# Holding back four chunks as two pairs with block products in a fused attention and mixer kernel

## Chip, cores and metric

The kernel runs on one core of a Trainium2 chip. The metric is device time in microseconds, the median of several executions. The four runs of the kernel before lie within 0.3% of each other, those of the changed kernel within 1.0%. All runs told here count as fast: none is more than 1.5% above the fastest run of the same kernel. The engines are TensorE (PE in the profile; PEld are its weight loads), VectorE (DVE), ScalarE (ACT), GpSimd (POOL), and the sync engine (SP), whose queue issues DMAs.

## The reference, cut to what matters

```python
# attention: 8 batches, 8 heads, 576 positions, 64 wide, with a bias by distance
scores = q @ k.T / 8 + bias[h]
attn   = softmax(scores)                       # in fp32
x      = heads_joined(attn @ v)                # (8, 576, 512)
# mixer, low rank over positions, then a feed-forward over channels
u   = x + (x.T @ U @ V).T                      # U: 576x32, V: 32x576
out = u + relu(u @ w_ch1) @ w_ch2              # 512 -> 2048 -> 512
```

## The kernel before

Attention goes by groups: a group is one pair of heads of one batch, 32 in all, numbered from 0. From group 4 on a loop runs each group in three segments. Each segment issues scores and exps, a share of feed-forward matmuls as filler, and products with v (a bias product multiplies exps by exp of the bias, on VectorE). The feed-forward works on nine chunks of 512 tokens: chunks 0 to 7 are the first 512 tokens of a batch, chunk 8 gathers the eight remainders of 64. From chunk 1 on the second product of a chunk is a block product with seven multiplications (Strassen's scheme in Winograd's form) inside a chunk; for the last two chunks together the first product is one as well.

```python
for g in range(NPAIR, NG):                     # groups 4 to 31
    for seg in range(3):
        emit_held(g, seg)                      # DMA transposes of q and k that are due
        ...                                    # scores and exps
        if 3 * g + seg < 6 * NPAIR + 5:
            work.even(6 * NPAIR + 5 - 3 * g - seg)
        else:
            work.run(2.1)                      # us of feed-forward matmuls as filler
        ...                                    # mixing, bias products, products with v
```

q and k are loaded as tiles of 128 x 512. From batch 3 on, DMA transposes on SP's queue turn them into qkT, ten for a batch. They are put into the program at a fixed place:

```python
def load_tasks(b):
    g0 = b * NPAIR
    due = max(3 * (g0 - 3) + 1, now[0] + 2)    # segments: group g0-3, its second one

def emit_held(g, seg):                         # at most two in a segment
    while held and (held[0][1] <= g or (held[0][0] <= now[0] and n < 2)):
        held.pop(0)[2]()
        n += 1
```

A relu of the first product goes to ScalarE if more than 1.5 us of filler have been issued in its segment, else to VectorE. Sums of weight blocks for the pair (fold_w1, sixteen) are made by VectorE in the last eight groups.

The softmax here doesn't subtract the row's maximum and nothing guards it: scores larger than these inputs give would overflow.

Of the kernel before, what the change touches and what calls it, by code (L numbers as in the profile page):

```python
# [36 lines left out]
def kernel(  # L37
# [34 lines left out]
    qbp = ctx.enter_context(tc.tile_pool(name="qbp", bufs=16))  # L72
# [61 lines left out]
    uT = [const.tile([128, NPAIR, S0], FP16, name=f"uT{i}") for i in range(3)]  # L134
    u_rem = const.tile([128, 4, NPAIR, 128], FP16)
    uT_rem = const.tile([128, NPAIR, S0], FP16)

    def rem_heads(t):
        return t.rearrange("p (a two d) -> p a two d", two=2, d=D)

# [114 lines left out]
    def first_cast(st, cast):  # L255
        qb = qbp.tile([128, 512], BF16, name="qb")
        cast(
            out=qb.rearrange("p (j h d) -> p h j d", j=4, h=2),
            in_=st.rearrange("p (h j d) -> p h j d", h=2, j=4),
        )  # L260
        return qb

    def first_qk(which, pr):
        qb = qbp.tile([128, 512], BF16, name="qb")
        first_load(which, 2 * pr, 2 * pr + 2, qb, nc.gpsimd)
        return qb

    def load_main(b, which, t):
        src = (q, k, v)[which]
        if which < 2:  # L270
            tl = qbp.tile([128, 512], BF16, name="qb")
            dst = tl.rearrange("p (h d) -> p h d", h=H)
        else:
            tl, dst = None, v_bf[b % 2][:, t, :, 0:64]
        nc.gpsimd.dma_start(  # L275
            out=dst,
            in_=src[b, :, t * 128 : (t + 1) * 128, :].rearrange("h p d -> p h d"),
        )
        return tl

    def load_rest(which, t):
        tl = qbp.tile([128, 512], BF16, name="qb")
        nc.gpsimd.dma_start(
            out=tl[:, 0:384].rearrange("p (h d) -> p h d", d=D),
            in_=(q, k)[which][2, 2:H, t * 128 : (t + 1) * 128, :].rearrange(
                "h p d -> p h d"
            ),
        )
        return tl

    def load_pair(b, which, pr):
        tl = qbp.tile([128, 512], BF16, name="qb")
        dst = tl.rearrange("p (j h d) -> p j h d", j=4, h=2)
        for hh in range(2):
            nc.gpsimd.dma_start(
                out=dst[:, :, hh, :],
                in_=(q, k)[which][b, 2 * pr + hh, 0:S0, :].rearrange(
                    "(t p) d -> p t d", p=128
                ),
            )  # L300
        return tl
# [103 lines left out]
    def first_product(j, tail, g, after):  # L405
        rhs = uT[j % 3] if j < B else uT_rem
        for nt in range(NHT):
            gp_ = acc()
            for ct in range(4):
                nc.tensor.matmul(  # L410
                    gp_,
                    lhsT=w1b[:, ct, nt * 128 : (nt + 1) * 128],
                    rhs=rhs[:, ct, :],
                    start=(ct == 0),
                    stop=(ct == 3),
                )
                yield MM
            if (nt % 2) if tail else clock["seg"] > 1.5:
                nc.scalar.activation(g[:, nt, :], gp_, AF.Relu)  # L419
            else:  # L420
                nc.vector.tensor_relu(out=g[:, nt, :], in_=gp_)  # L421
            after(nt)

# [4 lines left out]
    def u_of(j, i, h):  # L428
        t, a = slice(2 * i, 2 * i + 2), slice(2 * h, 2 * h + 2)
        if j < B:  # L430
            return u_tok[j % 3][:, a, t, :].rearrange("p a t c -> p t a c")
        return u_rem[:, t, a, :]
# [19 lines left out]
    def plain_chunk(j, tail):  # L452
# [3 lines left out]
        for i in range(2):  # L456
            ob = osb.tile([128, 2, DM], FP32, name="ob")
            for t in range(2):
                ps = acc()
                c0 = 256 * i + 128 * t  # L460
                for nt in range(NHT):
# [13 lines left out]
                    in1=u_tok[j % 3][:, :, 2 * i + t, :],  # L475
                    op=ALU.add,
                )
            store(j, i, ob)

# [51 lines left out]
    def second_product(j, rows, between=lambda n: None, y_first=False):  # L531
# [56 lines left out]
        add(z, blk(1, 1), u_of(j, 1, 1))  # L588
        if y_first:
            y = bank()  # L590
            between(1)
            yield from half(y[:, 0, :], "a12", "b21", 0, True)
# [9 lines left out]
        store(j, 1, ob[1])  # L602
        if j < B:
            if y_first:
                yield from half(y[:, 1, :], "a12", "b21", 1, False)
            else:
                y = bank()
                yield from product(y, "a12", "b21", True)
            more(y, 0, 0)
        else:  # L610
            store_rem(1, ob[1])
            yield from late(0)
# [3 lines left out]
        if j < B:  # L616
            store(j, 0, ob[0])
        else:
            store_rem(0, ob[0], cols=slice(256, 512))
            yield from late(1)  # L620


    w1s = {}

    def fold_w1(i):
        m, q4 = divmod(i, 4)
        kt, h = divmod(q4, 2)
        lo = slice(512 * h, 512 * h + 512)
        hi = slice(1024 + 512 * h, 1536 + 512 * h)
        a11, a21 = w1b[:, kt, lo], w1b[:, kt, hi]  # L630
        a12, a22 = w1b[:, 2 + kt, lo], w1b[:, 2 + kt, hi]
        x, y, op = (
            lambda: (a21, a22, ALU.add),
            lambda: (w1s[1, kt, h], a11, ALU.subtract),
            lambda: (a11, a21, ALU.subtract),
            lambda: (a12, w1s[2, kt, h], ALU.subtract),
        )[m]()
        t = qbp.tile([128, 512], BF16, name="qb").bitcast(FP16)
        nc.vector.tensor_tensor(out=t, in0=x, in1=y, op=op)
        w1s[m + 1, kt, h] = t  # L640

    pb7, pb8 = uT[(B - 1) % 3], uT_rem
    t12 = uT[(B - 3) % 3]
    t34 = u_tok[(B - 3) % 3].rearrange("p a t c -> p a (t c)")

    def fold_u(i, ks):
        o = slice(ks.start, ks.stop)
        b1, b2 = slice(ks.start, ks.stop), slice(2 + ks.start, 2 + ks.stop)
        t1, t2 = t12[:, b1, :], t12[:, b2, :]
        out_, x, y = (  # L650
            (t1, pb8[:, b1, :], pb7[:, b1, :]),
            (t2, pb8[:, b2, :], t1),
            (t34[:, b1, :], pb8[:, b2, :], pb8[:, b1, :]),
            (t34[:, b2, :], pb7[:, b2, :], t2),
        )[i - 1]
        nc.vector.tensor_tensor(out=out_, in0=x, in1=y, op=ALU.subtract)

    flat = [p_sb[i].rearrange("p k h c -> p (k h c)").bitcast(FP16) for i in range(2)]
# [6 lines left out]
    def pair_chunk(sixth):  # L665
# [7 lines left out]
            [], [],  # L673
            v_bf[0].rearrange("p k h c -> p (k h c)").bitcast(FP16)[
                :, 0:2048
            ].rearrange("p (n c) -> p n c", c=256),
        )
        kept = [q32[1][:, 512 * i : 512 * i + 512] for i in range(5)]
# [5 lines left out]
        second7 = []  # L684
        x, y, z = {}, {}, {}

        def block(i, kt, n):
            c0 = (n if i in (11, 12) else 8 + n) * 128
            return w1b[:, kt + (2 if i in (12, 22) else 0), c0 : c0 + 128]
# [84 lines left out]
        for i in (3, 2, 4):  # L774
            fold_u(i, slice(1, 2))
# [18 lines left out]
        rest = second_product(B - 1, rows7, between, True)  # L794
# [19 lines left out]
        yield from second_product(B, rows8)  # L814
# [7 lines left out]
    class Work:  # L822
        def __init__(self):
            self.gens = [(0, plain_chunk(0, False))]
            self.gens += [(j, chunk(j, False)) for j in range(1, B - 2)]
            sixth = chunk(B - 2, False)
            self.gens += [(B - 2, head(sixth, 161)), (B - 1, pair_chunk(sixth))]
# [4 lines left out]
        def even(self, segs):  # L832
            self.run((128 * MM - self.done) / segs)
# [261 lines left out]
    def mix_h(g, hm=None):  # L1095
        b, pr = divmod(g, NPAIR)
        x, tt = x_pr[g], tt_pr[g]
        if hm is None:
            hm = acc()
        for t in range(4):  # L1100
# [9 lines left out]
            out=u_tok[b % 3][:, pr, :, :],  # L1110
# [4 lines left out]
        if on_pe(g):  # L1115
            return
        nc.sync.dma_start_transpose(
            out=uT[b % 3][:, pr, :].rearrange("c (t p) -> c t p", p=128),
            in_=u_tok[b % 3][:, pr, :, :].rearrange("p t c -> p (t c)"),
# [5 lines left out]
    def mix_ut(g, copy):  # L1125
# [16 lines left out]
        return lambda: copy(uT[b % 3][:, pr, :], tp)  # L1142

    def mix_rem(g, hr):
# [6 lines left out]
        def post():  # L1151
# [6 lines left out]
            if b % 2 == 0:  # L1158
                return
            r = b // 2  # L1160
            if b < B - 1:
                if pr < NPAIR - 1:
                    return
                prs = slice(0, NPAIR)
            elif pr == 0:
                return
            else:
                prs = slice(0 if pr == 1 else pr, pr + 1)
            nc.sync.dma_start_transpose(
                out=uT_rem[:, prs, r * 128 : (r + 1) * 128],  # L1170
                in_=u_rem[:, r, prs].rearrange("p a c -> p (a c)"),
            )
# [194 lines left out]
    pool_order = []  # L1367
    for g in range(NPAIR, NG):
        b, pr = divmod(g, NPAIR)
        for seg in range(3):  # L1370
# [20 lines left out]
            if 3 * g + seg < 6 * NPAIR + 5:  # L1391
                work.even(6 * NPAIR + 5 - 3 * g - seg)
            else:
                work.run(2.1)
# [9 lines left out]
            if g >= NG - 8 and seg:  # L1404
# [7 lines left out]
            elif seg == 1:  # L1412
# [6 lines left out]
                if b > 1 and pr == 1:  # L1419
# [22 lines left out]
    work.run(3.0)  # L1442
    mix_t_thin(g)
    work.run(0.7)
    turn(g)
# [3 lines left out]
    work.run(2.5)  # L1449
    fold_u(1, slice(0, 2))  # L1450
    work.run(1.7)
    for i in (2, 3, 4):
        fold_u(i, slice(0, 1))
    ready[B - 1] = ready[B] = True
# [31 lines left out]
```

## Time and profile before

| | before |
|---|---|
| time, median | 392.0 us |
| TensorE busy | 374.5 of 390.0 us |
| VectorE, ScalarE busy | 312.8, 222.5 us |
| start of group 10, of group 31 | 91.43, 306.70 us |
| from the start of group 31 to the end | 83.3 us |

The prediction shows the page and the windows. One thing it does not show matters later: how far ahead of their use the transposes go out. This is SP's queue in the kernel before; the columns are start, length, engine, line, operation, output and input, count. The ten transposes here are those of batch 4:

```profile
128.01 3.78 SPq L331 DMA_TRANSPOSE qkT<-rem  x2
131.89 2.52 SPq L331 DMA_TRANSPOSE qkT<-qb  x2
134.50 0.53 SPq L436 DMA_DIRECT2D out_dram<-ob  x1
135.13 2.71 SPq L331 DMA_TRANSPOSE qkT<-qb  x2
137.96 1.19 SPq L1117 DMA_TRANSPOSE uT<-u_tok  x1
139.25 5.92 SPq L331 DMA_TRANSPOSE qkT<-qb  x4
```

Batch 4 begins with the scores of group 16:

```profile
153.62 0.38 PE L951 MATMUL sc<-qkT 128*128 128x128 bf16 x4
```

The queue needs 17 us for the ten, with other transposes and a store in between; the last is issued by 145.2, and 8.4 us remain until it is needed. From the start of its issue to landing a transpose of q or k takes 5.3 us in the median; this last one, issued at 143.96, takes 6.3. So some 3 us are to spare. Nobody waits, and so nothing in a list of waits says how small the margin is.

### The profile page before, as it was taken

Reading aid. Unit: us, or ns where it says so; the run is one execution under the profiler, and the core shown is the slowest. Engines: PE = TensorE matmul, PEld = TensorE weight load, DVE = VectorE, ACT = ScalarE, POOL = GpSimd, SP = SyncE. Lnnn points to the kernel's source line nnn. Section 1 sums busy time; section 2 is a strip of 40 time slices with the busy share of each in tenths; the row PEclk is TensorE's granted clock in tenths of the full one; section 3 lists DMA queues with packets and bytes.
Section 4 is the critical chain, followed back from the end, with each engine's and each line's share of the span. In section 5 each row is a group of like instructions: output and inputs, shape, how many; then the busy total and the mean of one; then the engine's idle time right before and its main releaser. Section 6 shows DMA issues by size and latency. Waiting matters only on the chain.

```text
span 390.0 us, 10289 instructions
## 1 busy us (share of the span) xinstructions
PE 374.5 (96%) x4160; PEld 249.2 (64%) x4163; DVE 312.8 (80%) x692; ACT 222.5 (57%) x338; POOL 128.8 (33%) x187
## 2 busy tenths in 40 slices
PE   6889999999999999999999999999999999999995
PEld 5466556555568646875578556875587458644884
DVE  7866898879897688878788779878897797778873
ACT  5987555565655676556555665557655561488400
POOL 4998917553554055405530443222000000000000
PEclk9999999999999999999999999999999999999999
DMA  7999999999989799969989997969102101200023
GB/s 135 173 103 172 166 205 116 161 72 180 155 72 90 158 131 108 75 125 160 116 65 124 172 110 59 95 158 161 28 3 82 56 15 44 108 0 2 0 109 108
DMA packets 163542, 40.66 MB, mean 104 GB/s; under 512 B 151632, under 2 KB 159096, under 8 KB 163496
## 3 DMA queue, kind: packets, MB, share of 16 engines
q0 software_dynamic: 110304, 18.24, 65.8%
q1 hardware_dynamic: 51928, 20.86, 25.3%
q10 hardware_dynamic: 1264, 0.92, 0.9%
q8 instruction: 32, 0.52, 0.6%
q14 instruction: 14, 0.11, 0.1%
HBM read 37.84 MB, written 9.45 MB: 121 GB/s over the span
## 4 chain that ended last, share of the span: by engine, by line
PE 84%; DVE 10%; ACT 2%; DMA 1%; issue 1%; SPq 0%; ACTq 0%; DVEq 0%
PE acc L556 25%; PE acc L410 22%; PE o L1027 11%; PE sc L933 8%; PE acc L697 4%; PE acc L462 3%; DVE g L421 2%; PE sc L697 2%; PE acc L1101 2%; PE sc L951 2%; PE sc L972 1%; DVE p_sb L1003 1%; PE acc L907 1%; DMA stage<-in_q_dram 1%; DVE qkT L876 1%
## 5 line engine op out<-in xcount | busy, mean ns | idle before, releaser
L942 ACT ACTIVATE p_sb<-sc 128x1024 bf16<-128x1024 f32 (+1 forms) x125 | 120.3, 1015 | 95.0 <-PE sc L933 95.0
L410 PE MATMUL acc<-uT,w1b 128*128 128x512 f16 x448 | 106.6, 380 | 1.2 <-ACT g L419 0.7
L410 PEld LDWEIGHTS <-w1b 128*128 128x128 f16 x448 | 40.4, 98 | 53.8 <-issue 13.9
L1003 DVE TENSOR_TENSOR p_sb<-p_sb,eb 128x768 bf16<-128x768 bf16 (+4 forms) x156 | 65.7, 455 | 0.6 <-ACT p_sb L942 0.4
L421 DVE TENSOR_SCALAR g<-acc 128x512 f16<-128x512 f32 x78 | 52.2, 684 | 7.9 <-PE acc L410 6.8
L1027 PEld LDWEIGHTS <-p_sb 128*128 128x128 bf16 x1550 | 53.4, 97 | 4.6 <-issue 0.9
L1027 PE MATMUL o<-v_bf,p_sb 128*128 128x65 bf16 x1475 | 55.6, 193 | 0.2 <-DVE xp L1053 0.2
L933 PE MATMUL sc<-qkT 64*128 64x512 bf16 x256 | 40.2, 382 | 1.4 <-ACT p_sb L942 0.9
L1388 POOL COPY gate<-xp 1x2 bf16<-1x2 bf16 x18 | 3.5, 193 | 113.0 <-DVE xp L1053 113.0
L556 PEld LDWEIGHTS <-g 128*128 128x128 f16 x336 | 32.1, 98 | 9.2 <-issue 4.3
L556 PEld LDWEIGHTS <-stage 128*128 128x128 f16 x336 | 32.0, 98 | 8.4 <-issue 4.1
L1053 DVE TENSOR_TENSOR xp<-o,rcp 128x320 bf16<-128x320 f32 x60 | 29.5, 491 | 3.2
L275 POOL DMA_DIRECT2D v_bf<-in_v_dram x32 | 28.4, 915 | 1.7 <-issue 1.6
L556 PE MATMUL acc<-w2b,g 128*128 128x256 f16 x224 | 28.3, 273 | 0.6 <-DVE g L421 0.6
L556 PE MATMUL acc<-tw,stage 128*128 128x256 f16 x224 | 28.1, 273 | 0.5 <-DVE ob L426 0.5
L426 DVE TENSOR_TENSOR ob<-acc,u_tok 128x512 f32<-128x512 f32 x28 | 19.3, 688 | 9.9 <-PE acc L556 9.5
L419 ACT ACTIVATE g<-acc 128x512 f16<-128x512 f32 x34 | 20.4, 600 | 11.0 <-PE acc L410 10.8
L1109 DVE TENSOR_TENSOR u_tok<-acc,xp 128x512 f16<-128x512 f32 x31 | 21.3, 686 | 6.2 <-PE acc L1101 6.0
L575 DVE TENSOR_TENSOR ob<-acc,ob 128x512 f32<-128x512 f32 (+1 forms) x25 | 16.7, 666 | 7.9 <-PE acc L556 7.7
L983 ACT ACTIVATE p_sb<-sc 128x640 bf16<-128x640 f32 x31 | 21.7, 699 | 0.3 <-PE sc L975 0.3
L964 ACT ACTIVATE p_sb<-sc 128x512 bf16<-128x512 f32 x31 | 18.5, 597 | 4.6 <-PE sc L1148 1.0
L275 POOL DMA_DIRECT2D qb<-in_k_dram x20 | 18.2, 910 | 1.6 <-issue 1.6
(168 smaller groups left out, 571.0 us busy)
## 6 DMA issues: line engine op xcount, KB each, us to landing
out_dram<-ob SPq DMA_DIRECT2D x16, 512.0 KB, 3.1
v_bf<-in_v_dram POOLq DMA_DIRECT2D x32, 128.0 KB, 5.7
qb<-in_q_dram POOLq DMA_DIRECT2D x23, 128.0 KB, 3.9
qb<-in_k_dram POOLq DMA_DIRECT2D x23, 128.0 KB, 4.0
w1b<-in_moe_w_ch_dram POOLq DMA_DIRECT2D x4, 512.0 KB, 6.3
w2b<-in_moe_w_ch_dram POOLq DMA_DIRECT2D x2, 1024.0 KB, 13.7
qb<-in_q_dram POOLq DMA_DIRECT2D x10, 64.0 KB, 5.1
qb<-in_k_dram POOLq DMA_DIRECT2D x10, 64.0 KB, 4.1
```

Source lines behind the costliest of these rows:

```text
L275: nc.gpsimd.dma_start(out=dst, in_=src[b, :, t * 128 : (t + 1) * 128, :].rearrange("h p d -> p h d"),)
L410: nc.tensor.matmul(gp_, lhsT=w1b[:, ct, nt * 128 : (nt + 1) * 128], rhs=rhs[:, ct, :], start=(ct == 0), stop=(ct == 3),)
L421: nc.vector.tensor_relu(out=g[:, nt, :], in_=gp_)
L556: nc.tensor.matmul(ps, lhsT=left[a](n)[:, t * 128 : t * 128 + 128], rhs=right[b](n), start=first and n == 0, stop=n == 7, skip_group_check ...
L697: nc.tensor.matmul(ps, lhsT=lhs, rhs=rhs[:, kt, :], start=first and kt == 0, stop=kt == 1, skip_group_check=True,)
L933: nc.tensor.matmul(sp[:, hh, :], lhsT=kT[rows, i * 128 : (i + 1) * 128], rhs=qT[rows, 0:S0], start=True, stop=True,)
L942: nc.scalar.activation(P[:, i, hh, 0:S0], sp[:, hh, :], AF.Exp, scale=scale)
L983: nc.scalar.activation(P4[:, 0:SP], sp.rearrange("p a c -> p (a c)")[:, 0:SP], AF.Exp, scale=scale,)
L1003: nc.vector.tensor_tensor(out=t, in0=t, in1=e, op=ALU.mult)
L1027: nc.tensor.matmul(o[:, qt * 66 : qt * 66 + 65], lhsT=lhs[:, c0 : c0 + 128], rhs=rhs, start=(kt == NKT and qt == 0), stop=(kt == NKT - 1), ...
L1053: nc.vector.tensor_tensor(out=xo[:, :, hh], in0=o[:, :, 0:64], in1=rbc, op=ALU.mult)
L1109: nc.vector.tensor_tensor(out=u_tok[b % 3][:, pr, :, :], in0=hm.rearrange("p (t c) -> p t c", t=4), in1=x[:, 0:4, :], op=ALU.add,)
```

## The change

Intent: the first product of two more chunks (5 and 6) is to be done as a pair too, which saves 16 of 128 matmuls. For this, chunks 5 to 8 wait until the attention is over. Their mixed tokens need a fourth set of tiles, for which eight of the sixteen q and k tiles are given up after the first batches. The filler in the loop becomes an even share of what is left to do there. Cuts are marked.

```diff
-    qbp = ctx.enter_context(tc.tile_pool(name="qbp", bufs=16))
+    qbp = ctx.enter_context(tc.tile_pool(name="qbp", bufs=8))
+    early_qb = const.tile([128, 8, 512], BF16)       # q, k of the first batches,
+    late_u = early_qb.bitcast(FP16)                  # then the fourth set of mixed tokens
+    uT.append(late_u[:, 0:4, :])
+    u_tok.append(late_u[:, 4:8, :].rearrange("p a (t c) -> p a t c", t=NKT))
...
-            if (nt % 2) if tail else clock["seg"] > 1.5:
+            if (nt % 2) if tail else clock["seg"] > 0.9:
                 nc.scalar.activation(g[:, nt, :], gp_, AF.Relu)
...
+    pairs = [
+        Pair(B - 3, uT[(B - 2) % 4], uT[(B - 4) % 4],
+             v16[0].rearrange("p (a c) -> p a c", c=S0)),
+        Pair(B - 1, uT_rem, uT[(B - 3) % 4], uT[(B - 2) % 4]),
+    ]
...
+    def last_chunks(fourth):
+        rows = []
+        yield from pair_chunk(pairs[0], fourth, rows)
+        ...
+        sixth = second_product(B - 2, rows[0], between)
+        yield from head(sixth, 97)
+        yield from pair_chunk(pairs[1], sixth, rows)
+        yield from second_product(B, rows[1])
...
+    upto = 128 * MM + 4 * (64 * MM + 112 * HALF) - 10.5
-                work.run(2.1)
+                work.even(upto, 3 * NG - 3 * g - seg)
...
-            if g >= NG - 8 and seg:
+            if g >= NG - 4:
                 fold_w1(len(w1s))
```

The place at which the transposes are put (`due` above) is not touched.

## The prediction

> **What bounds the kernel now.** I read the page's busy shares first, then the 40 slices and the chain that ended last, then windows by stage, and last the order of single instructions in one turn of the attention loop.
>
> ```profile
> PE 374.5 (96%) x4160; PEld 249.2 (64%) x4163; DVE 312.8 (80%) x692; ACT 222.5 (57%) x338; POOL 128.8 (33%) x187
> ...
> PE   6889999999999999999999999999999999999995
> ...
> DVE  7866898879897688878788779878897797778873
> ...
> PE 84%; DVE 10%; ACT 2%; DMA 1%; issue 1%; SPq 0%; ACTq 0%; DVEq 0%
> ```
> TensorE (PE) is busy in every slice but the first and the last and carries 84% of the chain, VectorE (DVE) 10%. So time is TensorE work plus the gaps in it, and VectorE is the engine that makes gaps.
>
> ```profile
> 150.00:180.00 30.00, 30.00 (x369) 21.96 (x368) 25.10 (x54) 16.60 (x25) 9.90 (x15) 1.00 0.90 111
> ...
> 300.00:320.00 20.00, 19.37 (x215) 10.59 (x212) 16.83 (x37) 12.58 (x20) 0.00 (x0) 1.00 0.13 41
> 320.00:370.00 50.00, 49.96 (x363) 32.78 (x361) 40.16 (x71) 27.00 (x45) 0.00 (x0) 1.00 0.09 30
> 370.00:390.00 20.00, 15.15 (x137) 13.04 (x134) 10.62 (x17) 0.00 (x0) 0.00 (x0) 0.99 0.33 106
> ```
> Columns: stretch, length, busy time of PE, weight loads, DVE, ACT, POOL, then clock and DMA. The clock is 0.99 to 1.00, so no throttle. The tail that holds the existing pair of chunks (320 to 370) is gapless. All gaps together are 390.0 - 374.5 = 15.5 us: about 5.8 in the first 30 us (loading), 4.85 at the very end, some 5 in the attention loop.
>
> The loop runs one group (a pair of heads) in three segments; feed-forward matmuls fill it. Starts of five consecutive groups are the times of their remainder scores:
>
> ```profile
> 194.47 0.38 PE L951 MATMUL sc<-qkT 128*128 128x128 bf16 x4
> ...
> 204.43 0.38 PE L951 MATMUL sc<-qkT 128*128 128x128 bf16 x4
> ...
> 214.52 0.38 PE L951 MATMUL sc<-qkT 128*128 128x128 bf16 x4
> ...
> 224.64 0.38 PE L951 MATMUL sc<-qkT 128*128 128x128 bf16 x4
> ```
> A group takes 9.96 to 10.12 us here. The group from 184 us took 10.69; three others of groups 11 to 30 also took 10.65 to 10.89. In a quiet group 29 feed-forward matmuls of 0.216 are 6.27, so attention's own TensorE work is 10.09 - 6.27 = 3.82 us.
>
> **What the Trainium skill says.** "TensorE: Matmul & The Clock Gate", section "Wait — 56ns, not 53.3ns?", gives 215.7 ns start to start for a warm matmul of 512 columns. The trace agrees: in the tail, pairs of these start 0.43 us apart. So a removed one is worth 0.216 us while TensorE is full. "VectorE: DVE Perf Modes", section "The perf-mode tier table", says that tensor_tensor reading PSUM runs at 1x and in 16-bit SBUF at 2x. Agrees: 0.69 us for 512 elements from PSUM and 0.69 for 1024 in SBUF. "TensorE: Matmul & The Clock Gate", section "Architectural detail", says that VectorE and ScalarE are strict FIFO: a bunch of sums ahead of a relu delays it and its PSUM buffer. The trace shows such a wait:
>
> ```profile
> 307.30 2.11 PE L410 MATMUL acc<-uT,w1b 128*128 128x512 f16 x9
> 309.81 0.38 PE L410 MATMUL acc<-uT,w1b 128*128 128x512 f16 x1 [0.41 <-DVE g L421]
> 310.42 0.40 PE L1101 MATMUL acc<-tt,vpad 128*128 128x128 bf16 x4 [0.23 <-DVE g L421]
> ```
> "ScalarE: Activation LUTs", section "What ACT_TABLE_LOAD costs", gives 186 ns + 0.833 ns per element, 1.04 us for a 1024-wide exp; the trace has 1.015.
>
> **The change part by part.** Counts are from the built programs' instruction order.
>
> (1) Removed: a chunk's plain first product is 64 matmuls of 512 columns. Two chunks as a block product with seven multiplications take 7 x 2 x 8 = 112 in place of 128. Before, one of four pairs does so; after, two. Weight matmuls go from 560 to 544: 16 x 0.216 = -3.46 us of TensorE. Everything else on TensorE has the same count. This is the only work saved on the bound.
>
> (2) Moved: the filler in the loop. Before, it is 2.1 us per segment; after, an even share: 27.65 + 4 x 26.05 - 10.5 = 121.3 us up to the loop's end, 27.65 of it by segment 29, so 93.7 over 67 segments = 1.40. A group's TensorE time falls from 10.1 to 3 x 1.40 + 3.82 = 8.0 us. About two chunks' work moves behind the loop, where it runs gapless. The last exp, now near 316 us, should come near 316 - 22 x 2.05 = 271, plus new gaps. A move by itself saves nothing.
>
> (3) VectorE in the loop. A group's fixed work is five bias products (0.417 + 2 x 0.551 + 0.484 + 0.281 = 2.28), two reciprocals (0.38), two normalisations (0.98), one mix sum (0.69), one remainder sum (0.29): 4.62 us. Filler adds relus at 0.684, sums at 0.69, weight folds at 0.417. Before, the crowded groups have 4.62 + 5 x 0.684 + 4 x 0.69 = 10.80 against 10.1 on TensorE, and of the three such, two took 10.65 and 10.69 and the third 10.10, with 10.82 in its successor. After, the limit is 8.0, and the crowded groups, numbered from 0 to 31, are: 11 with 9.43; 18 with 4.62 + 4 x 0.684 + 4 x 0.69 = 10.12; 24 with 8.74; 28, 29, 30 with 8.61, 9.30, 9.99 (the twelve folds now sit in the last four groups, three each). VectorE instructions overlap a little, so I count 97% of the sums: excess 1.1, 1.8, 0.5, and 0.3 + 1.0 + 1.7. That is 6.4, from which three PSUM accumulators and lighter neighbours should absorb some 1.5 to 2. So about 4.7 us of gaps from group 10 on, against 3.5 before by the same reading (periods over 10.1 us). Cost: +1.2. In the first six groups the filler rate is unchanged, and the lower threshold (0.9 for 1.5) sends four more relus to ScalarE; there groups took up to 0.9 more than their TensorE work. I credit -0.4.
>
> (4) ScalarE. A group has 4 x 1.015 + 0.597 + 0.699 + 0.273 + 0.185 = 5.81, and 0 to 2 relus of 0.60: at most 7.0 of 8.0. The last segment of a group is tight: 2.03 + 0.19 of ScalarE against 0.54 + 1.40 + 0.14 = 2.1 of TensorE, but the next segment needs only 1.57. I put +0.4 on this.
>
> (5) The second pair. ScalarE gains 24 copies at 0.59, eight relus at 0.597, seven wide ones at 1.05 and loses twelve relus: +19 us. VectorE gains 24 x 0.69 + 5 x 0.426 and some 1.9 of folds and loses 20 x 0.684: about +7. All of it lies beside matmuls as in the tail now, where the same loops leave 0.04 us of gaps in 50. One gap is copied. After a pair the second product of its second chunk starts before its sums are ready:
>
> ```profile
> 374.28 1.91 PE L556 MATMUL acc<-w2b,v_bf 128*128 128x256 f16 x16
> 376.73 1.91 PE L556 MATMUL acc<-tw,stage 128*128 128x256 f16 x16 [0.54 <-DVE ob L426]
> ```
> With two pairs it comes twice: +0.54.
>
> (6) Half of the q and k tiles. From batch 3 on there are 8 instead of 16. A batch's eight tiles are loaded about two groups before their transposes go out, and the next batch's loads come after these, so the reuse should not wait. The DMA's last transfers for the new first pair are needed earlier than now only by batches long complete. 0.
>
> (7) The end (final second product, last stores) is the same: 0.
>
> Sum: -3.46 + 1.2 - 0.4 + 0.4 + 0.54 = -1.7. I shade this to -2.2, because such a large rearrangement was presumably made with the intervals tuned: 392.0 - 2.2 = 389.8 us.
>
> **The rivals.**
> A. TensorE's work only: no new gap anywhere, -3.5 or, with relief in the early groups, -4.5: 387.5 to 388.5. For it: 80% VectorE and 57% ScalarE over the span, and a tail without gaps. Against it: the groups counted above.
> B. VectorE becomes the bound of the loop: TensorE follows its 9 to 10 us in crowded groups with nothing absorbed. Then the gaps are 6.4 or more against 3.5, and with waits on PSUM buffers behind them perhaps 8: 391 to 394. For it: two of the 10.80 groups of before did take about 10.7. Against it: their neighbours had slack and took none of the excess.
> C. ScalarE's exps set the short segments: 0.2 us in each of 22 groups would be +4.4 on top, 393 to 395. Against it: 16.6 to 18 us of 30 now; that becomes about 78% of the loop.
> D. Loading is late: the loop turns 20% faster and has half the tiles. DMA shows 0.9 to 1.6 of its share in the loop, so a wait of 1 to 2 us per batch in five batches would give 395 and more. Against it: the waits now name no transfer on TensorE in the loop, and between bursts DMA drops to 0.03 to 0.5 (198 to 202 us, 208 to 220).
>
> **Range and chances.** The sure term is -3.5; the open ones are gaps between -1 and +6. This gives 386.5 to 394.0 for 8 in 10. Faster by over 2% needs less than 384.2, more than twice the work removed: 3%. Slower by over 2% needs 399.9, rivals C and D together: 3%. Within 2%: 94%.
>
> **What would show it.** 544 weight matmuls on TensorE and its busy time near 371. Last exp at 270 to 278 us. Groups of about 8.0 us, with groups 11, 18, 29 and 30 longer by 0.5 to 1.5 and their gaps ending on a VectorE relu, sum or normalisation. From the end of the loop a tail of about 110 us without gaps but for two of 0.5. Wrong if quiet groups take over 8.3 (ScalarE or loading), if crowded ones take 8.0 (rival A), if TensorE waits on a transfer, or if the pair waits for its copies.

## The result, and the profile after

The changed kernel takes 403.45 us (400.03 to 404.12, four runs) against 391.89: slower. The ratio is 1.0274, from 1.0214 to 1.0334. Ratios here are the mean time of one kernel's fast runs over that of the other's of the same rounds, so not quite the ratio of the medians that I quote. The range of the prediction, 386.5 to 394.0, does not hold it.

The page after:

```profile
PE 378.5 (94%) x4144; PEld 249.1 (62%) x4147; DVE 319.4 (80%) x702; ACT 236.7 (59%) x365; POOL 128.7 (32%) x187
...
PEclk9999999999999989999999999999999999999999
...
PE 59%; DVE 18%; DMA 7%; SPq 5%; ACT 5%; issue 4%; POOL 0%; ACTq 0%; DVEq 0%; POOLq 0%
PE acc L573 17%; PE acc L425 9%; DMA qkT<-qb 7%; PE o L1072 7%; PE acc L729 7%; SPq L346 5%; PE sc L978 4%; PE sc L729 3%; PE acc L478 3%; ACT p_sb L987 3%; DVE p_sb L1048 3%; DVE stage L520 2%; DVE g L436 2%; DVE xp L1098 2%; PE o L729 2%
```

TensorE has 16 instructions less, as planned, and yet is busy for 4 us more (371 us in all were predicted, 378.5 came). The lowered clock told below explains 1.7 of that; the rest was not looked into. The chain of what ended last now holds 12% of transposes: 7% of DMA into qkT and 5% of the queue that issues them (L346). Before, no transpose of q and k was in it. One slice has a lower clock.

The waits of TensorE in the loop, before and after (engine, line and what it waited for; total us, times, longest). Before:

```profile
PE acc L410 <- ACT g L419: 0.7, 1, 0.7
PE acc L907 <- DVE g L421: 0.6, 1, 0.6
PE acc L556 <- DVE g L421: 0.6, 1, 0.6
PE acc L1101 <- DVE g L421: 0.5, 1, 0.5
PE acc L1101 <- ACT g L419: 0.2, 1, 0.2
```

After:

```profile
PE sc L996 <- DMA qkT<-qb: 6.0, 6, 2.8
PE o L1125 <- DVE xp L1098: 1.0, 3, 0.5
```

The waits on relus are gone, and a new wait has come: the first scores of a batch wait for transposed q and k. The worst place is the start of batch 4, first on SP's queue, then on TensorE, then one line of the chain that ended last, in this stretch:

```profile
122.20 2.50 SPq L346 DMA_TRANSPOSE qkT<-rem  x2
124.80 6.18 SPq L346 DMA_TRANSPOSE qkT<-qb  x4
131.07 1.22 SPq L1163 DMA_TRANSPOSE early_qb<-early_qb  x1
132.38 5.66 SPq L346 DMA_TRANSPOSE qkT<-qb  x4
```
```profile
141.28 0.27 PE L996 MATMUL sc<-qkT 128*128 128x128 bf16 x2
142.08 0.23 PE L996 MATMUL sc<-qkT 128*128 128x128 bf16 x1 [0.53 <-DMA qkT<-qb]
145.08 0.23 PE L996 MATMUL sc<-qkT 128*128 128x128 bf16 x1 [2.77 <-DMA qkT<-qb]
...
145.53 2.83 PE L425 MATMUL acc<-uT,w1b 128*128 128x512 f16 x7
```
```profile
136.84 8.19 DMA qkT<-qb
```

Read them against the lines of before. The queue needs 16 us for the ten transposes (17 there), but group 16 comes 3.2 us after the last issue (138.04 to 141.28), not 8.4. The last transpose goes out at 136.84 and takes 8.19 us to land. With 5.2, the median of this kernel, it would have landed 0.8 us late, by estimate; the rest of the worst wait is slow landing. The traces show what it met: here the next loads of q and k go out from 138.1 on, while it is under way, and take 9.3 us to land themselves; in the kernel before they go out from 149.0 on, when the last two of the ten are about to land, and take about 4. After this pause the next seven filler matmuls start 0.4 us apart and not 0.22: the clock was lowered. In the window it reads 0.94 (the last but two of the numbers, ahead of DMA share and GB/s):

```profile
120.00:150.00 30.00, 26.63 (x341) 19.45 (x337) 19.89 (x46) 16.57 (x25) 10.27 (x15) 0.94 1.39 132
```

Three of the four runs have a mean clock of 0.994 to 0.996 and take 403.3 to 404.1; the one with 1.0 takes 400.0. So the lowered clock goes along with some 3.5 us. Not all of that is the clock's own: the trace has a granted clock of 0.50 from 145.90 to 149.31, which costs 1.7 us, and the run with 1.0 has no trace.

The rest of the difference is found by splitting the time at the starts of groups 10 and 31 (their remainder scores):

```profile
90.51 0.38 PE L996 MATMUL sc<-qkT 128*128 128x128 bf16 x4
...
273.45 0.38 PE L996 MATMUL sc<-qkT 128*128 128x128 bf16 x4
```

From the program order, filler between these two points is 132.1 us before and 88.3 after (matmuls of 512 columns at 0.216, of 256 at 0.109); attention's own work is 21 x 3.82 = 80.2 in both. What is over is lost. After the start of group 31 the changed kernel has 41.3 us more filler (111.9 against 70.6).

| us | group 10 to 31 | lost there | group 31 to the end | over what the filler says |
|---|---|---|---|---|
| before | 215.3 | 215.3 - 132.1 - 80.2 = 3.0 | 83.3 | |
| changed | 182.9 | 182.9 - 88.3 - 80.2 = 14.4 | 128.1 | 128.1 - 83.3 - 41.3 = 3.5 |

So 11.4 more in the loop, 3.5 more behind it, less 3.5 of matmuls saved: 11.4, and the medians differ by 11.6.

### The profile page after: what moved, and what is told of

It reads as the page before. It is cut to its first block, busy times and chain, and to the rows that moved or that the text cites. A ratio compares the mean times of both kernels' runs of the same rounds, so it can differ in the third digit from the quotient of the medians.

```text
span 401.5 us, 10315 instructions
## 1 busy us (share of the span) xinstructions
PE 378.5 (94%) x4144; PEld 249.1 (62%) x4147; DVE 319.4 (80%) x702; ACT 236.7 (59%) x365; POOL 128.7 (32%) x187
## 4 chain that ended last, share of the span: by engine, by line
PE 59%; DVE 18%; DMA 7%; SPq 5%; ACT 5%; issue 4%; POOL 0%; ACTq 0%; DVEq 0%; POOLq 0%
PE acc L573 17%; PE acc L425 9%; DMA qkT<-qb 7%; PE o L1072 7%; PE acc L729 7%; SPq L346 5%; PE sc L978 4%; PE sc L729 3%; PE acc L478 3%; ACT p_sb L987 3%; DVE p_sb L1048 3%; DVE stage L520 2%; DVE g L436 2%; DVE xp L1098 2%; PE o L729 2%
## 5 line engine op out<-in xcount | busy, mean ns | idle before, releaser
L425 PE MATMUL acc<-uT,w1b 128*128 128x512 f16 x256 | 63.8, 386 | 0.0
L436 DVE TENSOR_SCALAR g<-acc 128x512 f16<-128x512 f32 x58 | 39.3, 685 | 2.9 <-PE acc L425 2.1
L573 PEld LDWEIGHTS <-g 128*128 128x128 f16 x288 | 27.3, 98 | 8.7 <-issue 4.2
L573 PEld LDWEIGHTS <-stage 128*128 128x128 f16 x288 | 27.2, 98 | 8.3 <-issue 4.0
L573 PE MATMUL acc<-tw,stage 128*128 128x256 f16 x192 | 24.6, 273 | 1.1 <-DVE ob L442 1.1
L573 PE MATMUL acc<-w2b,g 128*128 128x256 f16 x192 | 25.1, 273 | 0.0
L716 ACT COPY qkT<-o 128x512 f32<-128x512 f32 x16 | 9.4, 588 | 24.1 <-PE o L729 24.1
L1155 DVE TENSOR_TENSOR u_tok<-acc,xp 128x512 f16<-128x512 f32 x24 | 16.5, 687 | 5.9 <-PE acc L1147 5.9
L996 PE MATMUL sc<-qkT 128*128 128x128 bf16 x128 | 13.4, 219 | 7.1 <-DMA qkT<-qb 6.0
## 6 DMA issues: line engine op xcount, KB each, us to landing
v_bf<-in_v_dram POOLq DMA_DIRECT2D x32, 128.0 KB, 5.6
qb<-in_q_dram POOLq DMA_DIRECT2D x20, 128.0 KB, 4.2
qb<-in_k_dram POOLq DMA_DIRECT2D x20, 128.0 KB, 4.2
```

The costliest lines, as they stand in the source:

```text
L425: nc.tensor.matmul(gp_, lhsT=w1b[:, ct, nt * 128 : (nt + 1) * 128], rhs=rhs[:, ct, :], start=(ct == 0), stop=(ct == 3),)
L436: nc.vector.tensor_relu(out=g[:, nt, :], in_=gp_)
L573: nc.tensor.matmul(ps, lhsT=left[a](n)[:, t * 128 : t * 128 + 128], rhs=right[b](n), start=first and n == 0, stop=n == 7, skip_group_check ...
```

## The experiments

Theory T: the loop turns 20% faster, but the transposes are put at a place counted in segments and take their time on SP's queue, so they come late. Rivals: H, the halved tiles delay loads; V, VectorE bounds the shorter groups; C, ScalarE does. The edits are shown shortened, without the counters that they need.

**Transposes two segments earlier.** Most later runs build on this kernel, called "early" below. Results are right.

```diff
-        due = max(3 * (g0 - 3) + 1, now[0] + 2)
+        due = max(3 * (g0 - 3) - 1, now[0] + 2)
```

> The changed kernel with the DMA transposes of q and k let go two segments earlier. Theory T (the faster loop leaves too little time for the transposes of a batch: TensorE waits 6.0 us for them in the changed kernel, and the clock falls after the longest wait): the waits on qkT fall from 6.0 us to under 2, the clock stays at 1.00, and the time falls by 5 to 9 us, to 394 to 398. Rival V (VectorE and ScalarE bound the shorter groups, the waits on transposes only take up time that would be lost anyway): under 2 us gained, 401 to 403. Rival H (halved tiles: the loads themselves come late): the transposes wait for their loads in the queue, under 3 us gained.

396.71 us, ratio 1.0115 (1.0088 to 1.0142): 6.7 faster than the changed kernel. TensorE waits for no transpose of q and k in the loop any more; its waits there, and SP's queue for batch 4:

```profile
PE o L1125 <- DVE xp L1098: 1.0, 3, 0.5
```
```profile
114.65 2.50 SPq L346 DMA_TRANSPOSE qkT<-rem  x2
117.26 2.68 SPq L346 DMA_TRANSPOSE qkT<-qb  x2
121.08 1.19 SPq L1163 DMA_TRANSPOSE uT<-u_tok  x1
122.36 8.78 SPq L346 DMA_TRANSPOSE qkT<-qb  x6
```

The last is issued by 131.1, and group 16 starts at 141.84, with four scores at once. The same eight tiles are there, so the loads were not late. T holds for these 6.7 us.

**No transposes at all.** The held transposes are dropped without being issued; wrong on purpose (scores are so small that the result still passes the comparison).

```diff
-            held.pop(0)[2]()
+            held.pop(0)
```

> The changed kernel without any DMA transpose of q and k from batch 3 on; wrong results on purpose. It bounds from above what these transposes cost. Theory T: all of the 6 to 7 us of waits and the 2 to 3 us of slow clock go, 393 to 395, and the groups after the tenth take 8.0 to 8.4 us each. Rival V: the groups stay at 8.7 on average and the time above 400.

396.61 us, ratio 1.0106. I had expected 393 to 395. Leaving them out gains no more than letting them go earlier: the early release removes all that they cost. It also shows that 4.7 us over the kernel before have another cause.

**Halved tiles alone, in the kernel before.** The new rule for tiles is put into the kernel before, with its sixteen sums of weights half in the lasting tiles.

```diff
-    qbp = ctx.enter_context(tc.tile_pool(name="qbp", bufs=16))
+    qbp = ctx.enter_context(tc.tile_pool(name="qbp", bufs=8))
+    early_qb = const.tile([128, 8, 512], BF16)       # and new_qb() as in the change
```

> The kernel before with only the tiles halved as in the change (8 lasting ones for the first batches, later 8; the weight sums keep 16). Theory T: the halving does nothing by itself, 391 to 393.5. Rival H: reuse of tiles delays loads and transposes, 395 to 401, with waits of TensorE on qkT.

391.96 us, ratio 0.9987 (0.9959 to 1.0016). H falls: halving costs nothing at the old pace, and "early", with the same eight tiles, shows that it doesn't force late transposes at the new one.

**The pace alone, in the kernel before.**

```diff
-                work.run(2.1)
+                work.run((121.3 - 128 * MM) / 67)
```

> The kernel before with only the filler of the loop cut from 2.1 to 1.40 us per segment, so that the loop turns at the changed kernel's pace and the rest runs behind it; wrong results on purpose, since mixed tokens are overwritten before their chunk is done. All 16 tiles are there and no second pair. Theory T: the same late transposes, 398 to 403, with 4 to 8 us of waits on qkT. Rival H or a fault in the second pair: 391 to 394 and no such waits.

407.43 us, ratio 1.039. TensorE waits 3.7 us on qkT, with sixteen tiles and no second pair, so a faster loop by itself makes the transposes late. The time is above the range, and not all from there: this kernel also waits 3.9 us for mixed tokens (uT), which its three sets give it late. It supports T in kind, not in size. The same transposes cost 2.3 us of waits less here than in the changed kernel; no run says why.

**A control: transposes earlier in the kernel before.** The same edit as the first.

> A control: the kernel before with its transposes let go two segments earlier. It shows no wait of TensorE on qkT, so the same time within 0.7 us, 391.3 to 392.7. A gain here would mean that the earlier release helps in some way other than the waits that it removes.

392.4 us, ratio 0.9997 (0.9976 to 1.0019). Where nothing waits for the transposes, letting them go earlier gains nothing.

Open now were the 4.7 us between "early" and the kernel before. By the split above, "early" takes 91.08 to 266.80 for groups 10 to 30:

```profile
91.08 0.38 PE L996 MATMUL sc<-qkT 128*128 128x128 bf16 x4
...
266.80 0.38 PE L996 MATMUL sc<-qkT 128*128 128x128 bf16 x4
```

That is 175.7, so 7.2 lost in the loop (before: 3.0), and 128.0 from group 31 on, the same 3.5 too many. All the following edits are made to "early", one thing each; where one builds on another of them, it is said.

**VectorE spared** two of five bias products a group from group 10 on; wrong on purpose.

```diff
-                band(g, 1)
+                if g < 10:
+                    band(g, 1)                # and so for band(g, 2)
```

> On the kernel with the transposes let go earlier (396.7), VectorE is spared two of the five bias products in each group from the tenth on: 1.10 us of 8; wrong results on purpose. Theory V (what is left of the loss in the loop, some 4.6 us, is VectorE running at its limit in groups of 8 us): 3 to 5 us faster, 392 to 394. Rival C (ScalarE's exps and small copies on the way from one segment to the next): under 1 us, 395.5 to 397.

395.24 us, ratio 1.0087. 1.5 us gained from 1.10 x 21 = 23 us less work, between the two ranges and hardly clear of noise (the intervals overlap). In the trace 0.5 of it lies in the loop, where one wait of 0.6 on a transpose has come back. V as the main cause falls.

**ScalarE spared** half of each main exp from group 10 on; wrong on purpose.

```diff
-                    P[:, i, hh, 0:S0], sp[:, hh, :], AF.Exp, scale=scale
+                    P[:, i, hh, 0:w], sp[:, hh, 0:w], AF.Exp, scale=scale   # w = 256 from group 10 on
```

> On the same kernel, ScalarE is spared half of each of the four main exps from group 10 on, 0.43 us each, 1.7 us a group; wrong results on purpose. Theory V: under 1.5 us faster, 395 to 397, since VectorE's work is the same. Rival C: 3 to 5 us faster, 392 to 394.

391.88 us, ratio 1.0012. 4.8 us gained, all in the loop: groups 10 to 30 take 171.0, so 2.5 are lost there, as little as before. ScalarE's side of a group, which I had put at +0.4, is most of what the transposes leave. Whether by its load or by its order, the edit alone doesn't tell; the traces do. First "early" (group 17, TensorE, then ScalarE), then this run (TensorE):

```profile
150.62 0.22 PE L1020 MATMUL sc<-qkT 128*128 128x128 bf16 x1
150.98 0.23 PE L1136 MATMUL sc<-ident,tT 128*128 128x128 bf16 x1
```
```profile
148.42 1.94 ACT L987 ACTIVATE p_sb<-sc 128x1024 bf16<-128x1024 f32 x2 [0.76 <-PE sc L978]
150.24 0.60 ACT L434 ACTIVATE g<-acc 128x512 f16<-128x512 f32 x1
150.72 0.21 ACT L1132 CAST tT<-o 128x32 bf16<-128x32 f32 x1
```
```profile
148.66 0.22 PE L1021 MATMUL sc<-qkT 128*128 128x128 bf16 x1
148.72 0.22 PE L1137 MATMUL sc<-ident,tT 128*128 128x128 bf16 x1
```

The matmul of the second line reads tT, the small cast (32 columns wide) with which ScalarE ends a group's mix, and in "early" this cast stands behind two exps and a relu. So the matmul starts 0.36 us after the one before it and not 0.06. In groups 10 to 30 such late starts add up to 2.8 us at this matmul (9 groups) and to 2.7 at the scores of 512 columns just before (L1017), which in ten of the groups wait for an exp; with short exps they are 0.4 and 0.2, in the kernel before there are none. That is about the 4.7 us. No list of waits shows them, since each counts there as less than 0.15 us, and such waits are left out. ScalarE is busy for 115.5 of 170 us in this stretch (90 to 260), so it is not the sum of its work that binds, but how much of it comes together at the end of a group, ahead of the cast. No run changes this order alone.

**Sums of weight blocks on GpSimd.** Results are right.

```diff
-        nc.vector.tensor_tensor(out=t, in0=x, in1=y, op=op)
+        nc.gpsimd.tensor_tensor(out=t, in0=x, in1=y, op=op)
```

> On the same kernel, the sixteen sums of weight blocks run on GpSimd, which is idle from 250 us on, in place of VectorE (16 x 0.417 = 6.7 us, twelve of them in the last four groups). Results are right. If VectorE's crowding at the loop's end makes the waits of 0.6, 1.0 and 0.6 us on normalisations and on a block sum there (273 to 292 us), 1.5 to 3 us faster, 394 to 395.5. If GpSimd is slow or holds VectorE up[...], the same or slower, 396 to 399.

409.8 us, ratio 1.0465: 13 us slower. The trace shows why, GpSimd first, then VectorE, then TensorE:

```profile
234.02 4.50 POOL L668 TENSOR_TENSOR qb<-w1b 128x512 f16<-128x512 f16 x4
238.46 4.47 POOL L668 TENSOR_TENSOR qb<-qb,w1b 128x512 f16<-128x512 f16 x4
242.89 4.71 POOL L668 TENSOR_TENSOR rem<-w1b,qb 128x512 f16<-128x512 f16 x4
```
```profile
232.80 13.80 DVE L1048 TENSOR_TENSOR p_sb<-p_sb,eb 128x768 bf16<-128x768 bf16 x2
```
```profile
246.66 0.35 PE L1072 MATMUL o<-v_bf,p_sb 128*128 128x65 bf16 x3 [10.50 <-DVE p_sb L1048]
```

GpSimd was free, ran ahead of the loop and did twelve sums at once, 1.1 us each. Two bias products of VectorE, 1.0 us otherwise, took 13.8 us, the second alone 13.0: it was done at 246.60, after eleven of the twelve sums. TensorE waited 10.5, and its clock was 0.50 from 240.3 to 250.5. The Trainium skill has this on "SBUF — State Buffer", section "Who interferes with whom": a VectorE instruction with two SBUF inputs contends with a GpSimd instruction that reads SBUF, and the ports that they share are an exclusive lock. The trace agrees and adds a size: VectorE didn't get in between eleven GpSimd instructions in a row. This run tells nothing of what the sums cost on VectorE.

**More relus on ScalarE**: the threshold from 0.9 to 0.6.

```diff
-            if (nt % 2) if tail else clock["seg"] > 0.9:
+            if (nt % 2) if tail else clock["seg"] > 0.6:
```

> On the same kernel, a relu goes to ScalarE once 0.6 us (0.9 in the change) of filler has run in its segment: more relus on ScalarE, fewer on VectorE; right results. Theory V: 1 to 3 us faster. Rival C: the exps wait behind relus, 1 to 3 us slower. Both at once: within 1 us.

398.36 us, ratio 1.0162: 1.7 slower, as C has it.

**None on ScalarE** from group 10 on.

```diff
-            if (nt % 2) if tail else clock["seg"] > 0.9:
+            if (nt % 2) if tail else clock["seg"] > (0.9 if g < 10 else 99):
```

> On the same kernel, no relu goes to ScalarE from group 10 on (in the change, those after 0.9 us of filler do). The kernel with more relus there (threshold 0.6) was 1.7 us slower. If ScalarE's chain is what is short, 1 to 3 us faster; if both engines are full by now, VectorE's 16 further relus cost as much, within 1 us or slower by up to 2.

397.72 us, ratio 1.0135 (1.0110 to 1.0160), not clear of the 1.0115 of "early" (1.0088 to 1.0142): about 1 us slower, within noise, and no gain. In the traces the loop takes 175.7 us in both, so relieving ScalarE at VectorE's cost brings nothing.

**The small cast at a group's end on VectorE** from group 10 on.

```diff
-        nc.scalar.copy(tT[g % 2][:, 0:R], tp[:, 0:R])
+        copy = nc.scalar.copy if g < 10 else nc.vector.tensor_copy
+        copy(tT[g % 2][:, 0:R], tp[:, 0:R])
```

> On the same kernel, the small cast of the 32-wide mix (0.185 us) that ends a group on ScalarE, behind two exps, goes to VectorE from group 10 on; TensorE's transpose at the start of the next group waits for it by 0.3 us in many groups. ScalarE chain: 1 to 4 us faster, at most 0.3 us a group less 0.2 of VectorE. VectorE bound: slower by 1 to 3, as the cast now waits behind bias products and relus.

399.53 us, ratio 1.0186: 2.8 slower. TensorE now waits 3.4 us for this cast, which stands behind other work on VectorE. No shift of work between the two engines gained, and of the three thresholds tried none beats that of the change.

My next theory was that the last segment of a group is too short: 0.7 us of attention matmuls and 1.4 of filler against two exps of 1.94. Four kernels tried to mend it, all with right results.

**Filler shared unevenly.**

```diff
-                work.even(upto, 3 * NG - 3 * g - seg)
+                work.even(upto, (3 * NG - 3 * g - seg) / (0.75, 1.0, 1.25)[seg])
```

> On the kernel with the transposes let go earlier (396.7): the filler of a group is shared 0.75, 1.00, 1.25 over its three segments in place of evenly, because the last one holds only 0.7 us of attention matmuls beside two exps of 1.94 together. Right results. If ScalarE's chain through that short segment makes the rest of the loss (the short exps gained 4.8), 1.5 to 3.5 us faster, 393 to 395. If VectorE does, no change within 0.7.

397.32 us, ratio 1.0142: no gain over "early".

**And relus on ScalarE only in first segments**, on top of the uneven shares.

```diff
-            if (nt % 2) if tail else clock["seg"] > 0.9:
+            if (nt % 2) if tail else clock["seg"] > (     # from group 10 on
+                    0.2 if seg == 0 else 99):
```

> As the one before, and from group 10 on relus go to ScalarE only in the first segment of a group, where it has 1.57 us of other work, and to VectorE in the two with exps. ScalarE theory: another 0.5 to 2 us faster, 392 to 394. VectorE theory: slower by up to 1 us in the segments that lose the help.

396.93 us, ratio 1.0132: none either.

**With larger differences of the shares**, on top of both.

```diff
-                work.even(upto, (3 * NG - 3 * g - seg) / (0.75, 1.0, 1.25)[seg])
+                work.even(upto, (3 * NG - 3 * g - seg) / (0.6, 1.0, 1.4)[seg])
```

> As the one before, with shares of 0.60, 1.00, 1.40. By the count of matmul time the segments are then 2.4, 2.7 and 2.7 us. ScalarE theory: as fast or up to 1 us faster; if first segments then have too little for VectorE to catch up with its bias products, slower by 1.

399.84 us, ratio 1.0205: slower.

**And the weight sums spread over five groups**, on top of the second of these four.

```diff
-            if g >= NG - 4:
+            if g >= NG - 5 and (seg < 2 or g >= NG - 2):
```

> As the second of these, with the twelve sums of weight blocks spread over the last five groups (2, 2, 2, 3, 3) in place of four. If VectorE's crowding there is worth anything after the other edits, 0.3 to 1 us faster; otherwise the same.

396.87 us, ratio 1.0133: no difference from the second.

That theory falls: by more than noise no variant beats "early", and the most even one is 3 us slower. What I had left out, by the trace, is a chain in the first segment; no run changes it alone. In the second of these kernels ScalarE does a small cast, two exps and a copy in order, and the mixing matmul needs the copy (ScalarE's lines first):

```profile
208.48 0.18 ACT L1133 CAST tT<-o 128x32 bf16<-128x32 f32 x1 [0.21 <-ACT p_sb L988]
208.79 0.60 ACT L1010 ACTIVATE p_sb<-sc 128x512 bf16<-128x512 f32 x1
209.28 0.70 ACT L1029 ACTIVATE p_sb<-sc 128x640 bf16<-128x640 f32 x1
209.87 0.27 ACT L1139 COPY tt<-sc 128x128 bf16<-128x128 bf16 x1
```
```profile
208.86 1.03 PE L425 MATMUL acc<-early_qb,w1b 128*128 128x512 f16 x4
210.19 0.38 PE L1148 MATMUL acc<-tt,vpad 128*128 128x128 bf16 x4 [0.31 <-ACT tt L1139]
```

From the cast to the end of the copy it is 208.48 to 210.14, 1.7 us, and only the filler of this segment hides it. Less filler there shows the wait.

**No sums of weight blocks** ("early" with plain blocks in their place; wrong on purpose).

```diff
-        nc.vector.tensor_tensor(out=t, in0=x, in1=y, op=op)
-        w1s[m, kt, h] = t
+        w1s[m, kt, h] = blk(11)
```

> On the kernel with the transposes let go earlier (396.7), the sixteen sums of weight blocks are left out and plain blocks multiplied in their place; wrong results on purpose. After the last group starts, this kernel and the changed one lose 3.5 us more than the kernel before, with waits of 0.6 and 1.0 us on normalisations and 0.6 on a block sum at the junction of loop and first pair. If VectorE's folds there are the cause, those waits shrink and the time falls by 2 to 3.5 us, 393.2 to 394.7. If only the copied gap behind a pair and the loop count, under 1 us.

394.78 us, ratio 1.0059: 1.9 gained. The changed kernel waits three times at the junction of loop and first pair:

```profile
279.57 0.93 PE L1072 MATMUL o<-v_bf,p_sb 128*128 128x65 bf16 x25 [0.61 <-DVE xp L1098]
...
283.46 0.29 PE L1125 MATMUL o<-upad,xp 128*128 128x32 bf16 x5 [1.01 <-DVE xp L1098]
...
298.56 0.59 PE L729 MATMUL acc<-uT,qb 128*128 128x512 f16 x2 [0.59 <-DVE g L749]
```

Without the sums, only the middle one stays:

```profile
275.75 0.29 PE L1124 MATMUL o<-upad,xp 128*128 128x32 bf16 x5 [1.04 <-DVE xp L1097]
```

So crowding of VectorE by these sums makes about half of the 3.5 us lost behind the loop. The range began at 2 us gained, so this is just below it. The wait that stays has no like in the kernel before; with the second gap behind a pair (0.54) it is about the size of the other half, but no run removes it.

**One pair at the same pace.** "Early" with the same chunks held back, but chunks 5 and 6 run singly and only the last two as a pair; results are right.

```diff
-            fourth = chunk(B - 4, False)
-            self.gens += [(B - 4, head(fourth, 161)), (B - 3, last_chunks(fourth))]
+            self.gens += [(B - 4, chunk(B - 4, False)), (B - 3, one_pair())]
...
+    def one_pair():
+        yield from chunk(B - 3, True)
+        sixth = chunk(B - 2, True)            # then its folds, head and
+        ...                                   # pair_chunk(pairs[1], sixth, rows)
```

> On the kernel with the transposes let go earlier (396.7): the same held-back chunks and the same loop, but chunks 5 and 6 run singly with plain first products and only the last two as a pair, with the folds moved behind the sixth chunk's first product; right results. Sixteen more matmuls of 0.216. If the second pair pays what its matmuls say, 3.5 us slower, 399.5 to 401. If its junctions and folds give it back (3.5 us more lost in the tail than before), no more than 1.5 us slower, 396 to 398.2.

398.66 us, ratio 1.0168 (1.0154 to 1.0182): 2.0 slower than two pairs, between the two ranges. The second pair brings 2.0 of the 3.46 us of its matmuls; 1.5 are given back. In this kernel the wait on a block sum (0.59) and one of the two gaps behind a pair (0.54) are not there.

**Both reliefs together**: short exps and no weight sums; wrong on purpose.

> The short exps and the missing weight sums together on the kernel with the transposes let go earlier; wrong results on purpose. Singly they gained 4.8 and 1.9. If the account is complete (late transposes, ScalarE's chain, VectorE's folds, and 3.5 us of matmuls saved under them), they add up: 389 to 391, below the kernel before. If something else is lost, 391.5 or more.

389.58 us, ratio 0.9939 (0.9927 to 0.9951). The two gains add up (4.8 + 1.9 = 6.7 off 396.7 is 390.0) and the kernel ends 2.4 us below the kernel before. That the saving of the second pair comes to light here is not shown by this alone, since the kernel before was not run with the same two reliefs. In the loop 261.70 - 90.20 - 88.3 - 80.2 = 3.0 us are lost, as before. This kernel isn't a version to use; no right kernel that I ran beats the kernel before, and the best of the changed line is "early" at 396.7.

## Why the prediction was wrong

The direction and the size were wrong: 389.8 was predicted, -2.2 us, and +11.6 came. Against the terms of its sum:

- Part (1), -3.46 us of matmuls: right as work. 16 instructions are gone. At "early" the second pair is worth 2.0.
- Part (2), the pace: right as TensorE's work, 8.0 us a group, but only five of the groups 10 to 30 run at it in "early" (7.8 to 8.0); the median is 8.3. The last exp starts at 281.8 in the changed kernel, outside the 270 to 278 of the prediction, and at 275.2 in "early".
- Part (6) is the step that failed. It asked if tiles would be free again in time, found yes, and put 0. That much is right in time (halving alone: 391.96), though a load on GpSimd did wait once, 5.4 us, for transposes to free its tile. But it never asked when the transposes go out and how long SP's queue takes for them. They cost 6.7 us with the lowered clock. "If TensorE waits on a transfer" was one of the prediction's own signs of being wrong, and it came: 6.0 us. Rival D named a wait of 1 to 2 us a batch and was given next to no weight, because no wait on a transfer stood in the profile before. It had the size (6.0 us over five batches) by luck, since it put it down to late loads and half the tiles. A margin leaves no wait, and this one was 8.4 us against 5.3 of landing.
- Part (4), ScalarE, was put at +0.4 and is the second step that failed. Halved exps gave 4.8, and the loss in the loop was 7.2 in "early" against 3.0. Rival C had told this size (+4.4, from exps in the short segments) and was argued away by busy sums. The prediction had even seen the tight place, the last segment (2.03 + 0.19 against 2.1), and mis-sized it: the small cast and an exp come late behind other work of ScalarE, and TensorE starts late by 5.5 us in all, though ScalarE is busy only 115.5 of 170 us.
- Part (3), VectorE, was put at +1.2 - 0.4 and counted groups 11, 18 and 28 to 30 as crowded. In "early" group 18 takes 8.95 and group 11 takes 8.18, and groups 28 to 30 take 8.30, 8.18 and 8.66: half of the excess or less came. Group 24 alone took more than told, 9.12. The 3.5 us of gaps that the kernel before was credited with are 4.2 by the same reading of its starts, 1.3 of them in group 10. Sparing VectorE 23 us gained 1.5.
- Part (5), the second pair's gap of 0.54, is there as told (0.54 twice). Not told were the waits at the junction of loop and first pair, 2.2 us in sum, of which 1.2 go without the weight sums.

Summed up: -3.46 for the matmuls, +6.7 for late transposes and the clock behind them, +4.2 more lost in the loop (mostly ScalarE), +3.5 behind it gives +10.9 of the 11.6 measured.

What stays open: what makes the wait of 1.0 us on a normalisation behind the loop, why the sum falls short of 11.6 by 0.7, and what a right kernel with ScalarE's work in a better order would gain.

## What to carry to other kernels

When a change makes a loop faster, list everything that is placed a fixed number of steps ahead (transposes, loads, prefetches) and compare its lead in microseconds, at the new pace, with queue time plus landing time; a margin that is used up shows in no list of waits before. Busy sums per turn say that an engine isn't full, not that its order fits: follow the chain from exp to copy to matmul inside the shortest stretch, by the starts of single instructions, since many small waits stand in no list. And work put on an idle engine isn't free if it holds up a busy one, as the weight sums on GpSimd did.

## What the Trainium skill lacked or had wrong

- "DMA: Bandwidth & Descriptors", section "DMA Transpose (X-bar)": no time for a transpose in SBUF as the queue sees it. Here one of 128 x 512 (2-byte) takes 1.22 us of SP's queue and 5.2 us to land, both in the median, and up to 9.2 beside loads of q and k; ten for a batch fill the queue for 16 us with what lies between.
- "TensorE: Matmul & The Clock Gate", section "What's actually happening": it lets the clock fall after an idle window of some 3.4 us. Here the longest pause was 2.77 us (142.31 to 145.08), and in the 3.41 us before the clock fell (142.49 to 145.90) TensorE was busy for 0.82; the granted clock was then 0.50 for 3.41 us. So the window need not be wholly idle; how much work it may hold, neither the section nor these runs tell. In one of four runs of the same kernel the mean clock stayed at 1.0.
- "SBUF — State Buffer", section "Who interferes with whom": it calls the shared ports an exclusive lock and doesn't say whether the other engine gets in between two instructions. Here VectorE did not over eleven GpSimd instructions in a row: 13.0 us for one bias product of some 0.5. By the record that product had begun 0.4 us before the first of the sums (233.60 and 234.02), and it lost all the same; whether this speaks against the page's rule that the first to issue holds the ports is not shown, since spans on GpSimd are rough.
